# A scan with a mixture of adapters on one core: the store of chunks 68 and 69 from two DMA queues

## The chip, the cores and the metric

The kernel runs on one core of a Trainium2 chip. The metric is the time of one execution on the device in microseconds (us), less being better. SyncE (SP) issues the DMAs; 16 DMA engines move the data between HBM and the on-chip memory SBUF. TensorE (PE) multiplies, VectorE (DVE), ScalarE (ACT) and GpSimd (POOL) do the rest.

## The reference

Two inputs of 8 sequences x 6400 steps x 128 channels go through a linear recurrence along the steps, and each of the 51,200 resulting rows through a mixture of 8 low-rank adapters, of which the two with the largest logits count:

```python
for t in range(S):                      # a, b: (8, 6400, 128)
    h = a[:, t] * h + b[:, t]
    x[:, t] = h
logits = x @ w_gate                     # x as (51200, 128), w_gate (128, 8)
topk = argpartition(-logits, 2)[:, :2]
w = softmax over the two chosen logits
out = x + sum over the chosen e of  w_e * ((x @ A[e]) @ B[e])     # A (8, 128, 16), B (8, 16, 128)
```

Inputs and output are 32-bit floats. `a` and `b` are 26.2 MB each, the output is 26.2 MB.

## The kernel before, in words

The rows are cut into 100 chunks of 512 rows. A chunk is `J` = 4 blocks of 128 rows. The stages of a chunk:

- **Load** (`load`, line 710): SyncE loads `a` and `b` for two chunks at once, 512 KB a DMA, into six pairs of buffers `a_tm` and `b_tm`. A buffer is loaded again when TensorE has read it.
- **Front** (`front`, lines 731, 749, 787): TensorE transposes `a` and `b` so that the channels lie on the partitions, ACT copies the transposed `a` to `a_st`, and DVE runs the recurrence as a scan into `xT`. The scans are one chain from chunk to chunk.
- **Logits** (`zlogits`, lines 807 and 813): TensorE multiplies six blocks (a unit) by the gate and by all the adapters' A side by side; ACT copies the result to `zl`.
- **Gating** (`gating`, lines 844 to 883): for a group of up to four units, GpSimd and DVE find the two largest logits, ACT takes the sigmoid (877) and DVE writes the weights `g` (883).
- **Back** (`back_part`): GpSimd (916) (for chunks 82, 84, 86 and 90 to 99 DVE, 920) multiplies `zl` by `g` into `zw`; TensorE transposes it (929); DVE or ACT copies it (938, 935); TensorE adds x and the adapters' output in PSUM (943, 944); ACT (958), for chunks 95 and 97 DVE (955), copies the sum to `outt`.
- **Store** (`store`, line 989): SyncE stores two chunks at once, 512 KB, from `outt`; the last four chunks go one by one, 256 KB each.

`outt` holds `NO` = 72 blocks, that is 18 chunks; chunk 86 writes where chunk 68 lay, and `olast` tells it which store it has to wait for.

No engine decides its order when it runs. A planner in the program (`Program.schedule`) simulates the five queues with an estimated duration for each operation, due times (`NUDGE`, a table of ranks by the operation's name) and the time of an issue (`ISSUE`), and fixes one order for each engine; where no operation that is due can go on, it takes the earliest that is ready. `Program.waits` then places the semaphore waits, and each engine works through its list in order.

A store is one DMA over 128 partitions, with 4 KB of each partition for two chunks. `SPLIT` makes an exception of the store that begins with chunk 68: `cuts` lists the numbers of partitions of its parts, `lows` where each begins, and `send` issues one DMA for each on SyncE, all with the same semaphore (`parts` counts them). At its end SyncE waits for the semaphores of the stores (`final`).

Of the kernel before, what the change touches and what calls it, by code (L numbers as in the profile page):

```python
# [10 lines left out]
PERIOD = 6  # L11
# [6 lines left out]
LAND_MARGIN = 1.0  # L18
Q_RATE = {3: 4.2e-3, 5: 2.1e-3, 7: 2.1e-3}
SCAN_SELF = 0.13  # L20
ISSUE = {"sp": 0.52, "act": 0.45}
LOAD_RATE = 387e3
STORE_RATE = 413e3
DMA_START = 0.3
# [191 lines left out]
}  # L216
WINDOW = {'pe': 0.0, 'act': 0.0, 'dve': 0.0, 'pool': 0.0, 'sp': 0.0}
START = (-999, "", 0)
# [22 lines left out]
NO = 72  # L241
TAIL = 0
STORE_TAIL = [1, 1, 1, 1]
SPLIT = {68: [124, 4]}
TOP8 = 4
TEMPLATE = {
    "la": [0.0, 0.0, 0.0],
# [50 lines left out]
class Program:  # L298
# [34 lines left out]
    def schedule(self):  # L333
# [17 lines left out]
        while any(queue.values()):  # L351
# [35 lines left out]
            else:  # L387
                free[e] = t + ISSUE[e]
                dma = max(dma, free[e] + DMA_START) + op.dur
# [57 lines left out]
def bass_associative_scan_2x2__then__mixture_of_adapters_kernel(  # L447
# [14 lines left out]
    J = C // 128  # L462
# [50 lines left out]
    for u0, n in groups:  # L513
        nb = sum(m for _, m in units[u0 : u0 + n])
        if pos + nb > NZ:
            pos = 0
        for u in range(u0, u0 + n):
            zpos[u] = pos
            pos += units[u][1]

    with ExitStack() as stack:
# [48 lines left out]
        P = Program()  # L570
        eng = {}

        def sem(name):
            return sb(nc.semaphore(name))
# [4 lines left out]
        def dma_sem(key):  # L579
            if key not in s_dma:  # L580
                s_dma[key] = sem("s_" + key)
            return key
# [11 lines left out]
        for key, dur, dst, src in (  # L594
# [6 lines left out]
                START, sem=dma_sem(key),  # L601
# [19 lines left out]
        def place_pick():  # L621
            with nc.allow_low_precision(reason="sums of a single one"):
# [18 lines left out]
                op=ALU.mult),  # L641
# [15 lines left out]
        o_la, o_lb, o_A, o_B, o_ae, o_sc = {}, {}, {}, {}, {}, {}  # L657
        o_Z, o_ze, o_mu, o_T, o_te, o_D, o_oe, o_st = {}, {}, {}, {}, {}, {}, {}, {}
        o_g = {}
        zlast, xlast, olast = {}, {}, {}  # L660

        def get(d, k):
            return [(d[k], True)] if k in d else []
# [238 lines left out]
        def back_part(gi, ch, c, b0, n):  # L902
# [45 lines left out]
            xlast[ch % NX] = o_D[c]  # L948
            o0 = b0 % NO
            freed = {olast[o0 + k].i: olast[o0 + k] for k in range(n) if o0 + k in olast}  # L950
            deps = [(o_D[c], True)] + [(x, True) for x in freed.values()]
            ov, bv = outt[:, o0 : o0 + n, :].rearrange("p k w -> p (k w)"), bank[:, 0 : n * 128]
            if c in OE_DVE:
# [4 lines left out]
                                lambda: eng["act"].copy(ov, bv), ba(gi, c, "oe"))  # L958
            for k in range(n):
                olast[o0 + k] = o_oe[c]  # L960

        def place(c):
            turn = c - (NCH - TAIL_CHUNKS)
            if turn < 0:
                return pO[:, c % 2, :], get(o_oe, c - 2)
            assert NCH - 1 in o_sc
            t = turn % 6
            if turn < 6:
                if t < 2:
                    free = get(o_oe, c - 2)  # L970
                elif t < 4:
                    free = get(o_ae, NCH - 2 + (NCH + t) % 2)
                else:
                    free = get(o_sc, NCH - 2 + (NCH + t) % 2)
            else:
                free = get(o_oe, c - 6)
            return (pO[:, (c if t < 2 else t) % 2, :] if t < 2 else (pA if t < 4 else pB)[:, t % 2, :]), free

        def store(c, m):
            q = c * J % NO  # L980
            r0 = rows[c]
            src = {olast[q + k].i: olast[q + k] for k in range(m * J)}
            dst = out[r0 : r0 + m * C, :].rearrange("(h p j) d -> p h j d", p=128, j=J)
            view = outt[:, q : q + m * J, :].rearrange("p (h j) d -> p h j d", j=J)
            cuts = SPLIT.get(c, [128])
            lows = [sum(cuts[:i]) for i in range(len(cuts))]

            def send():
                all = [eng["sp"].dma_start(dst[p : p + n], view[p : p + n]) for p, n in zip(lows, cuts)]
                return all if len(all) > 1 else all[0]  # L990

            op = P.add(
                "sp", f"st{c}", m * C * D * 4 / (STORE_RATE if m == 2 else LOAD_RATE), [(x, True) for x in src.values()],
                send, (PERIOD * (c // PERIOD), "st", c % PERIOD // 2),
                sem=dma_sem(f"st{q // (2 * J)}" if m == 2 else f"stx{c % 4}"), parts=len(cuts),
            )
            o_st[c] = op
            for k in range(m * J):
                olast[q + k] = op
# [20 lines left out]
        for gi, (u0, n) in enumerate(groups):  # L1020
            for u in range(u0, u0 + n):
                b0, m = units[u]
# [31 lines left out]
        @block.sync  # L1054
        def _(sp):
            run("sp", sp)
            final = {}
            for op in P.order["sp"]:
                if op.sem.startswith("st"):
                    final.pop(op.sem, None)  # L1060
                    final[op.sem] = op
            for key in final:
                sp.wait_ge(s_dma[key], 16 * sum(o.parts for o in o_st.values() if o.sem == key))

# [43 lines left out]
```

## Time and profile before

| What | Value |
|---|---|
| median of 3 runs | 203.14 us (202.98 to 203.28) |
| the profiled execution's own time | 202.69 us |
| its span, first to last instruction of the program | 200.7 us |
| busy: PE, DVE, ACT, GpSimd | 90%, 88%, 86%, 70% |
| SyncE's DMA queue, share of 16 engines' span | 99.2% |
| moved over the span | 79.26 MB, 395 GB/s |
| DMAs of GpSimd's queue | none |

The profile is of one execution. Its views are: the page (busy shares, 40 slices, DMA queues, the chain that ended last, the costliest groups, the DMA issues), tables of stretches of the span, the order of time of each engine with what ended its idle time, the instructions of one line with the time from a DMA's issue to its landing, and the waits. PEld is TensorE's weight load, L958 means line 958 of the kernel. A DMA issue is time of the issuing queue, not of the transfer.

### The profile page before, as it was taken

What the parts mean: (1) busy time and instruction counts of PE and PEld (TensorE: products, weight loads), DVE (VectorE), ACT (ScalarE), POOL (GpSimd) and SP (SyncE); (2) the same over time, 40 slices, a digit from 0 to 9 for tenths busy, and PEclk for the clock granted to TensorE, in tenths of its full rate; (3) what the DMA queues carried; (4) which work ended last, traced back from release to release, by engine and by line L of the source; (5) the groups of instructions that cost most, each with busy time, mean ns of one, the idle gap of its engine ahead of it and who ended that gap; (6) DMA issues with size and microseconds to landing.
All of it is one profiled execution on the core that took longest, in us unless ns stands there. A gap on an engine that the chain in (4) does not pass through costs nothing.

```text
span 200.7 us, 7490 instructions
## 1 busy us (share of the span) xinstructions
PE 180.8 (90%) x3128; PEld 157.9 (79%) x3128; DVE 176.5 (88%) x287; ACT 172.7 (86%) x317; POOL 140.5 (70%) x182
## 2 busy tenths in 40 slices
PE   6978999999999999899989999988879999998980
PEld 6868877888788888788878888877767887887860
DVE  1579999999999999999999999987888989999980
ACT  2548898999999998999899998986988998998971
POOL 1314559997888899797989798979678677744200
PEclk9999999999999999999999999999999999999997
DMA  5999999999999999999999999999999999999995
GB/s 213 382 391 389 412 406 411 398 416 407 406 410 414 405 411 412 416 411 407 408 414 408 409 418 407 407 411 414 410 413 411 410 414 410 404 384 379 352 371 225
DMA packets 30089, 79.26 MB, mean 395 GB/s; under 512 B 2664, under 2 KB 2920, under 8 KB 30056
## 3 DMA queue, kind: packets, MB, share of 16 engines
q1 hardware_dynamic: 29480, 78.39, 99.2%
q8 instruction: 25, 0.41, 0.8%
q10 hardware_dynamic: 576, 0.40, 0.6%
q14 instruction: 8, 0.07, 0.1%
HBM read 52.56 MB, written 26.21 MB: 393 GB/s over the span
## 4 chain that ended last, share of the span: by engine, by line
PE 21%; DVE 18%; DMA 13%; POOL 7%; ACT 3%; issue 2%; SPq 0%; DVEq 0%
DVE xT L787 9%; DMA b_tm<-in_b_dram 7%; DMA a_tm<-in_a_dram 6%; PE pZ L807 4%; POOL zw L916 4%; PE pA L731 4%; PE pB L731 3%; PE pO L929 3%; DVE zw L920 3%; PE pO L943 3%; PE pO L944 3%; DVE zwT L938 2%; ACT zl L813 1%; POOL L L846 1%; DVE g L883 1%
## 5 line engine op out<-in xcount | busy, mean ns | idle before, releaser
L787 DVE TENSOR_TENSOR_SCAN xT<-a_st,xT,pB 128x512 f16<-128x512 f32 x96 | 120.3, 1253 | 7.8 <-PE pB L731 3.7
L916 POOL TENSOR_TENSOR zw<-zl,g 128x512 f16<-128x512 f32 x87 | 92.0, 1068 | 21.9 <-DVE g L883 18.8
L731 PE MATMUL pB<-ident_f,b_tm 64*128 64x64 f32 (+1 forms) x752 | 68.3, 232 | 2.1 <-DMA a_tm<-in_a_dram 1.0
L731 PE MATMUL pA<-ident_f,a_tm 64*128 64x64 f32 (+1 forms) x752 | 68.2, 232 | 1.7 <-DMA b_tm<-in_b_dram 1.3
L749 ACT COPY a_st<-pA 128x512 f32<-128x512 f32 x100 | 59.9, 608 | 8.3 <-PE pA L731 5.9
L731 PEld LDWEIGHTS pA<-ident_f,a_tm 64*128 64x128 f32 (+1 forms) x752 | 55.7, 140 | 6.8 <-DMA b_tm<-in_b_dram 2.4
L813 ACT COPY zl<-pZ 128x816 f32<-128x816 f32 (+1 forms) x69 | 57.8, 838 | 3.7 <-PE pZ L807 3.5
L731 PEld LDWEIGHTS pB<-ident_f,b_tm 64*128 64x128 f32 (+1 forms) x752 | 55.2, 139 | 7.0 <-DMA a_tm<-in_a_dram 1.7
L958 ACT COPY outt<-pO 128x512 f32<-128x512 f32 x91 | 54.3, 609 | 3.3 <-PE pO L944 2.6
L943 PE MATMUL pO<-ident_h,xT 128*128 128x128 f16 x368 | 51.0, 221 | 0.5 <-ACT zwT L935 0.2
L944 PE MATMUL pO<-cst_h,zwT 128*128 128x128 f16 x368 | 50.3, 219 | 0.0
L943 PEld LDWEIGHTS pO<-ident_h,xT 128*128 128x128 f16 x368 | 40.7, 113 | 2.5 <-ACT zwT L935 0.4
L807 PE MATMUL pZ<-cst_h,xT 128*128 128x136 f16 x400 | 36.0, 225 | 6.4 <-ACT zl L813 2.7
L929 PE MATMUL pO<-ident_h,zw 128*128 128x128 f16 x368 | 35.5, 220 | 2.1 <-ACT outt L958 1.3
L944 PEld LDWEIGHTS pO<-cst_h,zwT 128*128 128x128 f16 x368 | 36.5, 99 | 0.0
L807 PEld LDWEIGHTS pZ<-cst_h,xT 128*128 128x128 f16 x400 | 26.3, 115 | 11.6 <-DVE xT L787 4.3
L938 DVE COPY zwT<-pO 128x512 f16<-128x512 f16 x72 | 29.2, 408 | 2.4 <-PE pO L929 2.0
L929 PEld LDWEIGHTS pO<-ident_h,zw 128*128 128x128 f16 x368 | 22.6, 97 | 6.2 <-issue 1.5
L846 POOL TENSOR_SCALAR L<-k 128x192 f32<-128x192 f32 (+2 forms) x15 | 12.2, 810 | 3.2 <-DVE k L844 2.0
L935 ACT COPY zwT<-pO 128x512 f16<-128x512 f16 x20 | 11.9, 603 | 1.3 <-PE pO L929 1.0
L787 DVE TENSOR_TENSOR_SCAN xT<-a_st,pB 128x512 f16<-128x512 f32 (+1 forms) x8 | 7.5, 937 | 4.9 <-ACT a_st L749 4.7
L853 POOL TENSOR_TENSOR L<-k,m 128x192 f32<-128x192 f32 (+2 forms) x17 | 8.5, 500 | 2.5 <-DVE m L851 2.4
(56 smaller groups left out, 110.8 us busy)
## 6 DMA issues: line engine op xcount, KB each, us to landing
a_tm<-in_a_dram SPq DMA_DIRECT2D x48, 512.0 KB, 13.2
b_tm<-in_b_dram SPq DMA_DIRECT2D x48, 512.0 KB, 13.3
out_dram<-outt SPq DMA_DIRECT2D x47, 512.0 KB, 13.4
a_tm<-in_a_dram SPq DMA_DIRECT2D x4, 256.0 KB, 4.2
out_dram<-outt SPq DMA_DIRECT2D x4, 256.0 KB, 3.6
b_tm<-in_b_dram SPq DMA_DIRECT2D x3, 256.0 KB, 4.8
out_dram<-outt SPq DMA_DIRECT2D x1, 496.0 KB
b_tm<-in_b_dram ACTq DMA_DIRECT2D x1, 256.0 KB, 3.5
```

Of the source, the lines that this page charges most:

```text
L731: last = eng["pe"].transpose(*args)
L749: lambda: eng["act"].copy(a_st[c % NA][:, :], pA[:, c % 2, :]), fr(c, "ae"))
L787: last = eng["dve"].tensor_tensor_scan(out=x[:, s0:s1], data0=a_st[c % NA][:, s0:s1], data1=pB[:, c % 2, s0:s1], initial=init, op0=ALU.mul ...
L807: last = eng["pe"].matmul(pZ[:, k // (n // 2), o : o + W], xblock(b0 + k), Awg_h)
L813: return eng["act"].copy(zl[:, zb : zb + n, :].rearrange("p (h k) w -> p h (k w)", h=2), pZ[:, :, 0 : n // 2 * W])
L846: lambda e: e.tensor_scalar(out=ll, in0=kk, scalar1=0.0, scalar2=-1.0e30, op0=ALU.is_ge, op1=ALU.mult))
L916: lambda: eng["pool"].tensor_tensor(out=wv, in0=zv, in1=gv, op=ALU.mult), ba(gi, c, "mu"))
L929: last = eng["pe"].transpose(ptile[:, k * 128 : k * 128 + 128], zz[:, k, :], ident_h[:, :])
L938: lambda: eng["dve"].tensor_copy(zt, ptile[:, 0 : n * 128]), ba(gi, c, "te"))
L943: eng["pe"].matmul(dst, xblock(b0 + k), ident_h[:, :], start=True, stop=False)
L944: last = eng["pe"].matmul(dst, zt[:, k * 128 : k * 128 + 128], B_h, start=False, stop=True)
L958: lambda: eng["act"].copy(ov, bv), ba(gi, c, "oe"))
```

## The change

The pair of chunks 68 and 69, 512 KB, went out from SyncE as two DMAs over partitions 0 to 123 and 124 to 127. Now SyncE stores partitions 0 to 67 in one DMA, and a new operation `sw68` on GpSimd stores partitions 68 to 81 and 82 to 127 in two DMAs. `sw68` waits for the same copies as the store, has the same rank in the plan (102.531 above the same base) and a semaphore of its own; the planner books 2.6 us for the transfer and 1.3 us of GpSimd's time. A new table `oside` lets the chunk that writes the same blocks of `outt` next wait for this operation too, and SyncE waits for its semaphore at the end. The rest of the diff is the table `NUDGE` with the one new entry, wrapped anew.

```diff
-ISSUE = {"sp": 0.52, "act": 0.45}
+ISSUE = {"sp": 0.52, "act": 0.45, "pool": 1.3}
...
+    ... "sw68": 102.531, ...
...
-SPLIT = {68: [124, 4]}
+SPLIT = {68: [68]}
+ASIDE = {68: [14, 46]}
...
-        zlast, xlast, olast = {}, {}, {}
+        zlast, xlast, olast, oside = {}, {}, {}, {}
...
             freed = {olast[o0 + k].i: olast[o0 + k] for k in range(n) if o0 + k in olast}
+            freed.update({oside[o0 + k].i: oside[o0 + k] for k in range(n) if o0 + k in oside})
...
             for k in range(n):
                 olast[o0 + k] = o_oe[c]
+                oside.pop(o0 + k, None)
...
             cuts = SPLIT.get(c, [128])
             lows = [sum(cuts[:i]) for i in range(len(cuts))]
+            if c in ASIDE:
+                p0 = sum(cuts)
+                views = []
+                for n in ASIDE[c]:
+                    views.append((dst[p0 : p0 + n], view[p0 : p0 + n]))
+                    p0 += n
+                side = P.add(
+                    "pool", f"sw{c}", 2.6, [(x, True) for x in src.values()],
+                    lambda: [eng["pool"].dma_start(d, v) for d, v in views], (PERIOD * (c // PERIOD), "st", c % PERIOD // 2),
+                    sem=dma_sem(f"sw{c}"), parts=len(views))
+                o_st[-c] = side
+                for k in range(m * J):
+                    oside[q + k] = side
...
+            for op in P.order["pool"]:
+                if op.sem is not None:
+                    final[op.sem] = op
```

58 rows, old and new, of the table NUDGE are left out of this document.

## The prediction

> **What bounds the kernel now.** I read the page first: the busy shares and the DMA rows (section 1 to 3), then the DMA issues (6).
>
> ```profile
> span 200.7 us, 7490 instructions
> PE 180.8 (90%) x3128; PEld 157.9 (79%) x3128; DVE 176.5 (88%) x287; ACT 172.7 (86%) x317; POOL 140.5 (70%) x182
> q1 hardware_dynamic: 29480, 78.39, 99.2%
> out_dram<-outt SPq DMA_DIRECT2D x47, 512.0 KB, 13.4
> out_dram<-outt SPq DMA_DIRECT2D x4, 256.0 KB, 3.6
> out_dram<-outt SPq DMA_DIRECT2D x1, 496.0 KB
> out_dram<-outt SPq DMA_DIRECT2D x1, 16.0 KB
> ```
>
> SyncE's queue (q1) fills the 16 DMA engines for 99.2% of the span: the kernel moves data nearly all the time. The last two rows are the store of chunks 68 and 69 in its two parts, 124 and 4 partitions; unlike the other stores they have no landing time behind them. The view gives one only where a semaphore got sixteen updates for each DMA. The updates themselves are in the trace, but no view lists them, so they have no row: this semaphore got 10 from these two DMAs, of which 8 come at 178.6 to 181.2 us, four and four, and two at the issues. I read that as 124 = 4 x 31 and 4 = 4 x 1: each of the two parts ran on four engines, where 128 partitions run on all 16.
>
> Then the end, by stretches of the span (the last two columns are the share of the 16 DMA engines that is busy, and GB/s) and by the issues and landings of the last four stores.
>
> ```profile
> 158.00:166.00 8.00, 7.38 (x144) 6.35 (x141) 6.97 (x11) 7.42 (x14) 6.11 (x8) 1.00 1.03 409
> 182.00:186.00 4.00, 3.26 (x50) 2.70 (x47) 3.77 (x13) 3.73 (x10) 1.13 (x2) 1.00 0.98 376
> 186.00:190.00 4.00, 3.74 (x60) 3.40 (x60) 3.83 (x20) 4.00 (x10) 0.96 (x5) 1.00 0.90 342
> 194.00:197.30 3.30, 1.85 (x24) 1.16 (x20) 1.23 (x3) 2.33 (x4) 0.00 (x0) 1.00 0.85 323
> 197.30:199.00 1.70, 0.00 (x0) 0.00 (x0) 0.00 (x0) 0.00 (x0) 0.00 (x0) 0.63 0.82 313
> 199.00:200.70 1.70, 0.00 (x0) 0.00 (x0) 0.00 (x0) 0.00 (x0) 0.00 (x0) 0.50 0.17 64
> 196.02 0.59 ACT outt L958
> L989 SPq DMA_DIRECT2D out_dram<-outt x1: 351/351/351, 194.6 to 194.6; - x1
> DMA to landing us min/median/max: 3.7/3.7/3.7
> L989 SPq DMA_DIRECT2D out_dram<-outt x1: 854/854/854, 195.3 to 195.3; - x1
> DMA to landing us min/median/max: 3.7/3.7/3.7
> L989 SPq DMA_DIRECT2D out_dram<-outt x1: 1078/1078/1078, 196.2 to 196.2; - x1
> DMA to landing us min/median/max: 3.4/3.4/3.4
> L989 SPq DMA_DIRECT2D out_dram<-outt x1: 564/564/564, 197.3 to 197.3; - x1
> DMA to landing us min/median/max: 2.9/2.9/2.9
> ```
>
> The last copy (ACT L958) ends at 196.02 + 0.59 = 196.61, the last store is issued at 197.3 and lands at 197.3 + 2.9 = 200.2; the span ends 0.5 us later. The four landings are 198.3, 199.0, 199.6 and 200.2: a step of (200.2 - 198.3) / 3 = 0.63 us. One of these stores is 256 KB, 16 KB (16,384 bytes) for each engine, and at 409 / 16 = 25.6 GB/s for one engine that is 0.64 us. So the engine that lands last works without a break to the end: the bytes that it has left set the end, and the 0.7 us by which the last issue trails the last copy is hidden behind them. At the same time the share is 0.90, 0.85 and 0.82, so other engines are idle. The end belongs to a few late engines, which began the tail with more to do than the rest. The question of this change is who they are and what the new split gives them.
>
> **The change part by part.** *Bytes.* The pair is 512 KB, 4 KB a partition. Before, by the reading above, each of four engines gets 31 + 1 = 32 partitions, 128 KB or 131,072 / 25.6e3 = 5.1 us, and twelve get none. After, SyncE sends 68 partitions (68 = 4 x 17: 68 KB, 2.7 us each on four engines, 60 KB or 2.4 us less than before) and GpSimd's queue 14 + 46 = 60 partitions. No row shows a DMA from GpSimd. Its bounds on one engine are nothing and, for 46 partitions carried as 2 x 23, 92 KB or 3.7 us on each of two engines; the 14 would be one partition each, 4 KB or 0.16 us, on fourteen engines. Even spreading of the 60 over 16 is up to 4 partitions, 16 KB, 0.64 us for each. I take the first form, 2 x 23 and 14 x 1, as that is how the 124 behaved in this trace.
>
> The Trainium skill, "DMA: Bandwidth & Descriptors", section "Why a DMA increments its semaphore by 16 and not by 1", says the same for both queues: the largest count up to 16 that divides the slowest dimension, on SyncE's queue the lowest-numbered engines and on GpSimd's consecutive ones from a cursor that goes round. By it the 14 take engines 0 to 13 from a cursor at 0, and the 46 take 14 and 15. It adds an exception, in which GpSimd's DMAs take ceil(partitions / 16) on each engine, and a row on engines 7 and 15 being usually slower; no run here shows either.
>
> *Who was late.* The sixteen updates of the store before this one (issued 166.4; again without a row) come at 173.6 to 179.7: four within 0.3 us, three up to 175.1, two at 176.5 and 177.0, six at 178.2 to 178.4 and the last alone at 179.7. So some engines were 5 to 6 us ahead and one was 1.3 us behind the next, before the four got their 128 KB. Reading the following stores, the four that carried it were among the first seven; they join the late one, and at the end three or four engines land within 0.1 us at 200.2. Taking 2.4 us off the four therefore leaves the one that was late anyhow: it had none of the 512 KB, and it cannot get less. It gets 0 or 4 KB more: **0 to +0.16 us**, of which I take 0.16, since 14 of 16 engines would get such a piece.
>
> *SyncE's queue.* Two issues become one.
>
> ```profile
> 166.91 0.48 SPq L989 DMA_DIRECT2D out_dram<-outt  x1
> 167.43 1.76 SPq L989 DMA_DIRECT2D out_dram<-outt  x1
> 169.24 2.88 SPq L989 DMA_DIRECT2D out_dram<-outt  x1
> L989 SPq DMA_DIRECT2D out_dram<-outt x1: 372/372/372, 186.1 to 186.1; - x1
> 184.54 0.57 ACT L958 COPY outt<-pO 128x512 f32<-128x512 f32 x1
> ```
>
> An issue without congestion takes 0.37 us (the fourth row); these take up to 2.88 because the queue is full, so a dropped issue moves the wait to the next one. What follows in the queue are stores only, all loads went before. The buffer of chunks 68 and 69 is written next by chunk 86 (ACT at 184.54; its store goes at 186.1), 3.3 us after the last of the updates at 181.2, and the later buffers have similar room: **0**, unless the GpSimd part landed over 3 us later than now.
>
> *GpSimd.* The operation sw68 waits for the copies of chunks 68 and 69 and puts two DMAs into an engine that works in order. Behind it are the products zw (L916) and the gating of the next group, which releases ACT's sigmoid and DVE's g (L883), and DVE is the engine of the tail.
>
> ```profile
> 153.51 0.59 ACT L958 COPY outt<-pO 128x512 f32<-128x512 f32 x1 [0.50 <-PE pO L944]
> 156.92 3.09 POOL L916 TENSOR_TENSOR zw<-zl,g 128x512 f16<-128x512 f32 x3 [1.74 <-DVE g L883]
> 161.73 0.52 POOL L844 TENSOR_TENSOR k<-zl,m 128x192 f32<-128x192 f32 x1 [1.72 <-DVE m L862]
> 167.71 0.59 POOL L875 TENSOR_TENSOR k<-k,L 128x192 f32<-128x192 f32 x1
> 169.22 2.09 POOL L916 TENSOR_TENSOR zw<-zl,g 128x512 f16<-128x512 f32 x2 [0.92 <-DVE g L883]
> L916 POOL TENSOR_TENSOR zw<-zl,g x87: 1052/1062/1607, 16.8 to 182.1; 128x512 f16<-128x512 f32 x87
> ```
>
> Counted back from the last copy, chunk 69's is the first row, done at 154.1. GpSimd then sits idle for 1.74 us before 156.92 and 1.72 us before 161.73; from there to 168.3 it is busy nearly without a gap up to k of L875, which g waits for. The price of one issue lies between 0.37 us (SyncE's) and 1.6 us (the longest product of GpSimd), so two cost 0.7 to 3.2 us; the planner in the code books 1.3 for the operation's hold on the engine. I take 2 x 1.3 = 2.6 us, nearer to the engine's own rows. In an idle stretch 1.7 of it is covered and 0.9 is left; inside the busy stretch nothing is. DVE would feel that in full, but the end would not: the last store is issued 0.7 us after its copy because the issue before it takes 1.08 us, and that much delay is free. So 0.9 - 0.7 = 0.2 us at most from an idle stretch, and 2.6 - 0.7 = 1.9 us from the busy one. As the operation is ready by 154, I take the idle stretch, and as the products there have more than 3 us until their copies, **0**.
>
> The Trainium skill, "SBUF — State Buffer", section "Who interferes with whom", warns that GpSimd can be locked out of writing descriptors by certain DVE operations. The 87 products have a median of 1062 ns and a longest of 1607, so what this trace shows of such disturbance is 0.5 us once; by the rule the two issues could take longer than I book.
>
> *Sum.* 0.16 + 0 + 0 = +0.16 us. The profiled execution took 202.69 us, its span of 200.7 and 2.0 around it, 0.45 below the median of 203.14; it would become 202.85. On the median: 203.14 + 0.16 = **203.3 us**. A measurement of this kernel can tell about 0.2%, 0.4 us, from no change, so this counts as the same.
>
> **The rivals.** *A: the two engines of the 46 are not ahead (slower).* The 92 KB need 3.7 us of lead over the late engine. Of the sixteen, seven had over 4 us; nine had not. For an engine of the six, 1.3 us ahead, the end moves by 3.7 - 1.3 = 2.4 us; for the two with 2.7 and 3.2 us by 0.5 to 1.0, for the late one itself by 3.7. It decides as soon as the lead is under 3.7 us. In the middle +1.3: 204.4, at most 206.8. For it: nothing in the views says which engines are ahead, and the 14 partitions ahead of the 46 look neutral to it. Against: four light engines were hit by the 124, so the light ones seem to lie together. By the skill's row on engines 7 and 15 the late engine could be one of the two, the worst end of this rival.
>
> *B: GpSimd's DMAs spread evenly (slower by a little; the change then doesn't do what its numbers suggest).* Up to 4 partitions on the late engine: +0.64 us, 203.8. That is also the skill's exception.
>
> *C: GpSimd's two issues fall into the busy stretch (slower).* +0.2 to +1.9 us, in the middle 204.2. It decides when over 0.7 us reaches DVE. Against: the copies are done by 154 and two idle stretches follow.
>
> *D: the late engine is late because of the four (faster).* Then 2.4 us less on them frees the end until the last copy binds: issue at 196.65 instead of 197.3 saves 0.65 us, and a landing without a step of backlog another 0.64: -0.65 to -1.3 us, in the middle 202.2. For it: the share falls below 1 only after the four got their load, and they are among the last at the end. Against: the spread before the split.
>
> **How the numbers follow.** Forecast 0.35; A 0.24, B 0.09, C 0.10, D 0.22. The range reaches from the middle of D, 202.2, to 205.0, which holds B, C without its far end and A up to an engine with 1.8 us of lead; outside are A's worst and D's best, under 0.2 together. The forecast's own range is 202.9 to 203.5. Faster by over 0.2%: D, 0.22. Within 0.2%: the forecast, 0.35. Slower: A, B and C, 0.43.
>
> **What would show it.** Right: a queue of GpSimd's with 240 KB in section 3, the 272 KB store without a landing time, the last four landings again about 0.63 us apart and ending at 200.2 to 200.5, shares under 1 in the stretches from 182 us. A: landings after 200.7 with the last store issued at its old time, and loads that land later if the operation goes early. B: the late step of 0.6 us, with no two engines standing out. C: GpSimd's L875 of the group later than 167.71 and DVE's scans behind it. D: the last issue 0.04 us after its copy and a landing under 2.9 us. I am wrong on the main point if the last landing moves earlier by over 0.4 us, since by my reading no byte leaves the late engine.

## The result: 7.6 us slower, and the profile after

| | before | after |
|---|---|---|
| median (runs) | 203.09 us (202.98 to 203.28, 4) | 210.67 us (210.46 to 210.74, 4) |
| ratio, 95% interval | | 1.037 (1.035 to 1.039) |
| the profiled execution: own time, span | 202.69, 200.7 us | 210.74, 208.5 us |
| mean granted clock of TensorE | 0.993 | 0.982 |

The forecast was 203.3 us, the range up to 205.0: wrong, and by far. The kernel before ran again on the same chip beside each group of experiments; its medians were 203.2 to 203.5, and each difference below is against the one beside it. Ratios leave out runs that look disturbed by their clock; as in this kernel the clock falls because of its own gaps, all runs are listed where a group of them splits.

The page of after, and its table of DMAs:

```profile
span 208.5 us, 7488 instructions
PE 183.2 (88%) x3128; PEld 158.9 (76%) x3128; DVE 178.5 (86%) x287; ACT 173.2 (83%) x317; POOL 143.0 (69%) x184
q1 hardware_dynamic: 29356, 78.15, 95.5%
q0 software_dynamic: 416, 0.25, 0.4%
out_dram<-outt SPq DMA_DIRECT2D x4, 256.0 KB, 2.4
out_dram<-outt SPq DMA_DIRECT2D x1, 272.0 KB
out_dram<-outt POOLq DMA_DIRECT2D x1, 184.0 KB, 10.9
out_dram<-outt POOLq DMA_DIRECT2D x1, 56.0 KB, 5.7
```

q0 is GpSimd's queue. Its packets (in the trace, in no view) are 60 of 4 KB, 32 of 4 bytes and 324 of 8 bytes. The 56 KB DMA lands on all its engines within 0.9 us; in the other, two engines land at 167.6 and 167.8, 2 us behind the rest. So the split was as forecast: 14 single partitions, and 46 as 2 x 23, 92 KB on each of two engines. The small packets fit: 2 engines without any of the 14, one packet each, and 14 without any of the 46, 23 each, are 2 + 322 = 324. SyncE's queue (q1) no longer fills the span: 95.5% after 99.2%. Where it runs empty, by stretches (columns: PE, PEld, DVE, ACT, GpSimd busy with their instructions, clock, DMA share, GB/s):

```profile
158.00:166.00 8.00, 7.53 (x148) 6.71 (x147) 7.43 (x10) 7.20 (x13) 6.26 (x8) 1.00 1.04 406
182.00:186.00 4.00, 3.91 (x70) 3.31 (x71) 3.97 (x9) 4.00 (x10) 1.96 (x2) 1.00 0.92 347
186.00:190.00 4.00, 3.18 (x43) 2.44 (x43) 3.99 (x13) 3.53 (x8) 2.78 (x5) 1.00 0.48 187
190.00:194.00 4.00, 3.76 (x63) 3.39 (x62) 4.00 (x13) 3.78 (x9) 0.00 (x0) 1.00 0.61 230
194.00:198.00 4.00, 3.81 (x61) 3.24 (x58) 3.96 (x14) 3.33 (x9) 1.75 (x5) 1.00 0.47 179
202.00:205.22 3.22, 1.10 (x16) 0.76 (x14) 0.37 (x1) 1.59 (x3) 0.00 (x0) 0.85 0.41 151
```

From 186 to 198 us the share is 0.47 to 0.61, with DVE busy nearly all of that time. The end is no longer that of a late DMA engine: the last four stores, issued from 203.9 to 205.2, land at 205.9, 206.6, 207.3 and 208.0, each on all its engines within 0.2 us. Something in the last 50 us makes the engines late.

**Two places.** First the loads. SyncE's issues in before, then in after, and the load of `b` for chunk 92 (the second of each "x2") with the time to its landing:

```profile
151.42 1.80 SPq L710 DMA_DIRECT2D b_tm<-in_b_dram  x2
158.61 1.47 SPq L710 DMA_DIRECT2D a_tm<-in_a_dram  x1
160.12 0.67 SPq L710 DMA_DIRECT2D b_tm<-in_b_dram  x1
```

```profile
L710 SPq DMA_DIRECT2D b_tm<-in_b_dram x1: 596/596/596, 152.6 to 152.6; - x1
DMA to landing us min/median/max: 13.7/13.7/13.7
```

```profile
152.39 1.76 SPq L711 DMA_DIRECT2D b_tm<-in_b_dram  x2
159.43 3.03 SPq L711 DMA_DIRECT2D a_tm<-in_a_dram  x1
162.51 1.92 SPq L711 DMA_DIRECT2D b_tm<-in_b_dram  x1
```

```profile
L711 SPq DMA_DIRECT2D b_tm<-in_b_dram x1: 581/581/581, 153.6 to 153.6; - x1
DMA to landing us min/median/max: 16.1/16.1/16.1
```

The load takes 16.1 us instead of 13.7. Of its sixteen updates fifteen are there by 167.0 in after and the last at 169.7; in before 165.8 and 166.4. One engine is late. As I read it, it is one of the two that work on GpSimd's 4 KB packets until 167 us, in turn with the loads that were queued there before. The next issue hangs too, 3.03 us instead of 1.47. Who feels it in after, from the order of time of ACT, TensorE and DVE:

```profile
166.78 1.07 ACT L960 COPY outt<-pO 128x512 f32<-128x512 f32 x2 [1.13 <-DMA out_dram<-outt]
169.70 0.27 PE L732 MATMUL pA<-ident_f,a_tm 64*128 64x64 f32 x1 [1.32 <-DMA b_tm<-in_b_dram]
166.34 1.28 DVE L788 TENSOR_TENSOR_SCAN xT<-a_st,xT,pB 128x512 f16<-128x512 f32 x1 [0.47 <-PE pA L732]
170.59 1.28 DVE L788 TENSOR_TENSOR_SCAN xT<-a_st,xT,pB 128x512 f16<-128x512 f32 x1 [1.75 <-PE pB L732]
```

ACT waits 1.13 us for an earlier store that sits on the same engine (chunks 56 and 57, whose blocks it writes next), TensorE 1.32 us for the load, and between two scans of DVE's chain lie 4.25 us (before: 2.1). And TensorE's clock, before and after:

```profile
166.00:170.00 4.00, 3.84 (x68) 3.19 (x68) 4.00 (x7) 3.13 (x7) 2.88 (x4) 1.00 1.04 412
170.00:174.00 4.00, 3.81 (x79) 3.31 (x78) 4.00 (x8) 3.98 (x8) 3.04 (x5) 1.00 1.03 402
```

```profile
166.00:170.00 4.00, 1.36 (x27) 0.94 (x24) 2.37 (x4) 1.56 (x3) 2.82 (x5) 1.00 1.03 408
170.00:174.00 4.00, 4.00 (x56) 3.56 (x53) 2.75 (x3) 2.32 (x5) 1.21 (x2) 0.57 1.04 406
```

TensorE is busy in 1.36 of 4 us, and then runs at a mean clock of 0.57 for four. The trace's clock records, which no view lists, have it at 0.50 for one stretch of 3.41 us, from 170.1 to 173.5.

Second, the order. From chunk 77 on, the lists of all five engines differ from before: 30 places on TensorE, 25 on ACT, 41 on DVE, 8 on GpSimd, 2 on SyncE. The new operation's 2.6 us of transfer, booked on the planner's one DMA timeline, move every later landing that it plans with. Planned with 0 us of transfer and 1.3 us of GpSimd's time the order is that of before, and with 2.6 and 0 it is that of after: the transfer alone does it. The 2.6 is also far above what the planner books elsewhere: at its rate for stores (`STORE_RATE`, 413,000 bytes a us) the 240 KB would be 0.6 us, and planned with 0.6 the order is that of before too.

### The profile page after: what moved, and what is told of

Its sections match the earlier page's. It is cut to its first block, busy times and chain, and to the rows that moved or that the text cites. A ratio compares the mean times of both kernels' runs of the same rounds, so it can differ in the third digit from the quotient of the medians.

```text
span 208.5 us, 7488 instructions
## 1 busy us (share of the span) xinstructions
PE 183.2 (88%) x3128; PEld 158.9 (76%) x3128; DVE 178.5 (86%) x287; ACT 173.2 (83%) x317; POOL 143.0 (69%) x184
## 3 DMA queue, kind: packets, MB, share of 16 engines
q1 hardware_dynamic: 29356, 78.15, 95.5%
## 4 chain that ended last, share of the span: by engine, by line
DMA 21%; PE 17%; DVE 10%; ACT 7%; POOL 7%; issue 2%; SPq 1%; ACTq 0%; DVEq 0%
DMA b_tm<-in_b_dram 14%; DMA a_tm<-in_a_dram 7%; DVE xT L788 5%; POOL zw L917 4%; PE pZ L808 3%; PE pA L732 3%; PE pB L732 3%; PE pO L944 3%; PE pO L945 2%; PE pO L930 2%; ACT outt L960 2%; DVE zw L921 2%; ACT a_st L750 2%; ACT zl L814 1%; DVE zwT L939 1%
## 5 line engine op out<-in xcount | busy, mean ns | idle before, releaser
L944 PE MATMUL pO<-ident_h,xT 128*128 128x128 f16 x368 | 51.8, 222 | 1.1 <-ACT zwT L936 0.5
L945 PE MATMUL pO<-cst_h,zwT 128*128 128x128 f16 x368 | 51.0, 220 | 0.0
L808 PE MATMUL pZ<-cst_h,xT 128*128 128x136 f16 x400 | 36.5, 227 | 5.4 <-ACT zl L814 2.7
L808 PEld LDWEIGHTS pZ<-cst_h,xT 128*128 128x128 f16 x400 | 26.8, 115 | 10.6 <-DVE xT L788 4.6
```

Of the source, the lines that this page charges most:

```text
L808: last = eng["pe"].matmul(pZ[:, k // (n // 2), o : o + W], xblock(b0 + k), Awg_h)
L944: eng["pe"].matmul(dst, xblock(b0 + k), ident_h[:, :], start=True, stop=False)
L945: last = eng["pe"].matmul(dst, zt[:, k * 128 : k * 128 + 128], B_h, start=False, stop=True)
```

## The experiments

Three theories: ORDER (the new lists are slower), LOADS or ENGINES (the lump of 92 KB on two engines makes loads land late), START (a DMA of GpSimd's costs time at the start). In names such as T79 the letter is the operation (T the transposes of `zw`, P those of a chunk's `a` and `b`, `oe` the copy to `outt`, `te` the copy to `zwT`), the number the chunk.

**One cause at a time.** The order of before with the stores of after:

```diff
-        P.schedule()
+        P.schedule(); at = [o.name for o in P.order["pool"]].index("mu75"); P.order["pool"][at:at] = [o for o in P.ops if o.name.startswith("sw")]
...
```

(`mu75` is GpSimd's product of chunk 75. Two more lines, left out here, keep `sw68` out of the planning.)

> The planner's order of before on every engine, with the three stores of after (68 from SyncE, 14 and 46 from GpSimd, put ahead of the product of chunk 75 as in after). Theory ORDER (the new operation made the planner write another order for all engines from chunk 77 on, and that order is what is slow): most of the 7.6 us is gone; what is left is the 1.0 us offset of the start and about 2 us by which the last loads land late: 204.5 to 206. Theory ENGINES (23 partitions on each of two DMA engines make the last loads land 2.8 us late, and the tail magnifies that whatever its order): 209 to 211. Theory START (a queue of GpSimd's costs 1.0 us at the start): the first scans and stores are 1.0 us later than in before, here too.

Measured: 207.22, 207.29, 206.87 and 204.08 us, two levels, to which I come back. And the reverse, the order of after with the stores of before (sw68 is planned and then left out; `SPLIT = {68: [124, 4]}`):

> The planner's order of after on every engine, but GpSimd's operation is left out when the order stands, and SyncE issues 124 and 4 partitions as in before: no DMA from GpSimd. ORDER: about 5 us of the 7.6 stay, 207 to 209. ENGINES: 202.8 to 203.6, as before. START: the start is as in before, no 1.0 us offset.

Measured: 206.13 us (206.07 to 206.27), ratio 1.0142 (1.0118 to 1.0167): the new order alone costs 2.65 us, with no DMA from GpSimd and the loads landing as before (last 177.0, before 176.9). Neither theory alone holds the 7.6. How the order loses it, before and this kernel (ACT, then DVE):

```profile
169.12 0.59 ACT L958 COPY outt<-pO 128x512 f32<-128x512 f32 x1
169.61 0.84 ACT L813 COPY zl<-pZ 128x816 f32<-128x816 f32 x1
170.34 0.60 ACT L958 COPY outt<-pO 128x512 f32<-128x512 f32 x1
172.80 1.27 DVE L787 TENSOR_TENSOR_SCAN xT<-a_st,xT,pB 128x512 f16<-128x512 f32 x1
174.56 1.27 DVE L787 TENSOR_TENSOR_SCAN xT<-a_st,xT,pB 128x512 f16<-128x512 f32 x1
```

```profile
169.72 0.84 ACT L813 COPY zl<-pZ 128x816 f32<-128x816 f32 x1 [0.30 <-PE pZ L807]
171.29 1.08 ACT L958 COPY outt<-pO 128x512 f32<-128x512 f32 x2
172.42 1.06 POOL L916 TENSOR_TENSOR zw<-zl,g 128x512 f16<-128x512 f32 x1 [0.88 <-PE pO L929]
174.51 0.35 DVE L851 TENSOR_REDUCE m<-L 128x24 f32<-128x192 f32 x1 [0.49 <-POOL L L849]
174.78 1.27 DVE L787 TENSOR_TENSOR_SCAN xT<-a_st,xT,pB 128x512 f16<-128x512 f32 x1
176.29 1.27 DVE L787 TENSOR_TENSOR_SCAN xT<-a_st,xT,pB 128x512 f16<-128x512 f32 x1
```

The copies 77 and 76 stand behind other copies now and come one after the other from 171.29, instead of at 169.12 and 170.34; T79 needs the space in pO that they free, GpSimd waits for T79 0.88 us, DVE for GpSimd, and the same two scans come 2.0 and 1.7 us later. Is that first step a loss of its own? A plan with 1.3 us of transfer changes 17 places around it, and nothing later:

> No DMA of GpSimd, stores of before (124 and 4). The order is that which the planner writes when it books 1.3 us of transfer for the new operation instead of 2.6: 17 places differ from before, all around chunks 77 to 85 (TensorE: T79 behind the transposes of chunk 94; ACT: each of the copies 77 and 76 one place later; DVE: te79 two scans later), and the order after them is that of before. Theory FIRST STEP (the copies 77 and 76 that come 2.2 and 1.4 us late take pO from T79 and so the DVE chain; this loss is carried to the end): +1.5 to +2.0 over before, 204.6 to 205.5. Theory ALL OF IT (the 3 us of the new order come from the many changes in the last 20 us): under +0.5, 203.0 to 204.0.

Measured: 205.01 us (204.31 to 206.29), +1.8, ratio 1.0077 (1.0050 to 1.0103). FIRST STEP: by the medians two thirds of the order's 2.65 us. But the two slowest of the nine runs, 205.92 and 206.29, have the lowest clock (0.986 and 0.984). In the profiled one of them, 205.92, TensorE's clock falls behind the sparse stretch that the order makes, with no DMA from GpSimd:

```profile
170.00:174.00 4.00, 2.42 (x43) 1.73 (x41) 3.93 (x7) 2.79 (x6) 2.68 (x4) 1.00 1.03 405
174.00:178.00 4.00, 4.00 (x57) 3.60 (x54) 2.32 (x5) 2.80 (x5) 1.58 (x2) 0.57 1.03 394
```

Without these two the median is 204.68 us: the first step itself is nearer to 1.5 us, a little over half of the order's loss.

**The lump.** GpSimd's two DMAs in the other order, `ASIDE = {68: [46, 14]}`:

> As the first kernel of this call (order of before), but GpSimd stores 46 partitions first and then 14. If the DMA engines are dealt from a cursor, the 2 x 23 partitions now fall on other engines than in after. ENGINES: if the two are among those that run ahead, the loads land as in before, and the time is 203 to 204.5, clearly under the first kernel's; if they are late ones too, 209 to 211. ORDER: 203 to 206, within 2 us of the first kernel.

204.34 us (203.80 to 205.32), ratio 1.0051 (1.0028 to 1.0074): no lone late engine, the last load at 177.0. The same 60 partitions as one DMA, `ASIDE = {68: [60]}`:

> As the first kernel of this call (order of before), but GpSimd stores the 60 partitions in one DMA; 60 = 15 x 4, so 15 engines would carry 16 KB each instead of two 92 KB. ENGINES: the last load is at most 0.64 us late, 203 to 204.5. ORDER: the same, since only the 92 KB lump is gone and the order is that of before: 203 to 204.5. The difference to the first kernel is the price of the lump with the order unchanged: 0 to 2 us by ORDER, 5 to 7 us by ENGINES.

203.58 us, ratio 1.0009 (0.9985 to 1.0033): in this order no price can be measured, with GpSimd's DMA still there. It is the lump on two engines and, as I read the kernel before this one, which two; the trace does not number the engines.

Later in GpSimd's list, the lump meets few loads:

> Order of before, the three stores of after (68; 14 and 46), but GpSimd issues its two behind the product of chunk 83 instead of ahead of that of chunk 75, some 15 us later. Theory LOADS (the two 92 KB lumps cost time because their packets take half of an engine that still has loads queued): the last load lands as in before, within 0.5 us, and what is left is GpSimd's 1.9 us in a stretch with little idle time and the late engines' last stores: 203.8 to 205.5. Theory END (the lump costs its 3.7 us wherever it falls, at the end through the late engine's stores): 206.5 to 207.5, as with the early issue in the order of before.

204.79 us (204.57 to 205.43), ratio 1.0074 (1.0052 to 1.0095). The load of chunk 92 takes its 13.7 us again and the last one lands at 177.2: LOADS. The +1.6 left are GpSimd's issues in its busy stretch and late last stores; they were not taken apart. All parts from SyncE, `SPLIT = {68: [68, 14, 46]}`:

> Order of before; all three parts, 68, 14 and 46 partitions, from SyncE, which issues them behind the last load. LOADS: the loads land as in before whatever engines the lumps fall on; if they fall on the engines that carry the 68 anyhow (17 + 23 + 1 partitions, 164 KB on two of them against 128 KB before), these are ahead and 203.0 to 204.0 comes out. END: as the lump is there in full, 205 or more.

205.28 us, ratio 1.0098 (1.0063 to 1.0133), outside my 203 to 204: the loads are as in before (177.1), but one engine is 1.7 us behind the rest to the end and lands the last store at 202.7. So END has its share here, as I read it because the lump falls on SyncE's own four engines.

**The sum.** The kernel of after with 0 instead of 2.6 us booked, the same program as the first experiment:

> The kernel of after with one number changed: the planner books 0 instead of 2.6 us of transfer for the new operation. That alone gives back the order of before on every engine (GpSimd's 1.3 us stay booked). The program is that of the order of before with the new stores, whose four runs lay apart (204.08, and 206.87 to 207.29); this settles which is its time. ORDER and LOADS together (3.6 us each): 206.5 to 207.5, with now and then a run near 204 if the lump sometimes meets engines that are ahead. ORDER alone: 203.5 to 204.5 in nearly all runs.

205.04, 208.03, 204.39, 207.20, 206.99 and 208.46 us; ratio without the two of lowest clock 1.0128 (1.0079 to 1.0178). And the new order with GpSimd's 60 partitions in one DMA:

> The order of after (2.6 us booked), but GpSimd stores its 60 partitions in one DMA, so that no engine gets 92 KB. If the two causes add, what is left is the new order alone: 206.0 to 206.8, as with the stores of before in this order (206.13). If the new order is only slow because of a DMA from GpSimd at that place, 208 or more; if the lump was the whole cause, 203.3 to 204.

207.22 us (206.68 to 207.85), ratio 1.0183 (1.0159 to 1.0207), 0.4 above what was expected and +3.8 on before. So in this order even the one DMA is not free: the time is 1.1 us above that of the order alone, chunk 92's load takes 14.4 us instead of 13.7 there, and the last load lands at 178.5 instead of 177.0. By itself the order costs 2.65 us, and the lump, by the medians of two scattered sets of runs, 3.6 to 3.7. Together that is 6.2 to 6.4 of the 7.6 us; the other 1.2 to 1.4 come only with both, and no run takes them apart.

But why are there two groups of runs of one program? With the first experiment: 204.08 to 205.04 at clocks of 0.997 to 1.000, and 206.87 to 208.46 at 0.975 to 0.991. In the profiled run of 207.22 the load of chunk 92 lands after 16.7 us, and the clock falls; in that of 205.04 it lands after 14.6 us, and there is no drop of the clock:

```profile
166.00:170.00 4.00, 1.28 (x20) 0.85 (x18) 2.37 (x4) 1.56 (x3) 1.73 (x3) 0.94 1.05 410
170.00:174.00 4.00, 4.00 (x60) 3.56 (x58) 2.46 (x3) 2.80 (x6) 1.48 (x3) 0.63 1.02 401
```

```profile
166.00:170.00 4.00, 2.66 (x50) 2.22 (x51) 3.21 (x6) 2.15 (x5) 2.33 (x4) 1.00 1.03 408
170.00:174.00 4.00, 3.81 (x74) 3.33 (x72) 4.00 (x8) 3.98 (x8) 3.08 (x4) 1.00 1.04 412
```

TensorE is busy in 2.66 of 4 us, not in 1.28. What makes the lump hold up chunk 92's load less in one run than in another stays open: in both, GpSimd's DMA lands late (167.3 and 167.8 us), and so does the last load (179.8 and 179.3).

**The clock.** Transposes that nobody uses, to keep TensorE busy where it waits:

```diff
+        at = [o.name for o in self.order["pe"]].index("P94"); self.order["pe"][at:at] = [o for o in self.ops if o.name.startswith("fx")]
...
+        for k in range(12):
+            P.add("pe", f"fx{k}", 0.109, [(o_id, True), (o_sc[92], True)],
+                  lambda: eng["pe"].transpose(pB[:, 0, 0:128], ident_f[:, :], ident_f[:, :]), START)
```

> The kernel of after, unchanged but for 12 transposes of the identity into a free half of pB that TensorE runs ahead of the transposes of chunk 94, where it waits 1.3 us for the late load and where its clock then falls to 0.53 and 0.62 for four us. They keep TensorE busy and compute nothing that is used. Theory CLOCK (a good part of what the late loads cost is the clock that falls behind TensorE's idle time): the clock stays at 1.00 from 170 to 174 us and the time falls by 1.0 to 1.8 us, to 208.9 to 209.7. Theory WAIT (the late landing alone sets it): 210.4 to 211.5.

> As the one before this, with 24 instead of 12 of these transposes. CLOCK: the clock stays up and the time is that of 12 plus what the longer row of transposes delays TensorE beyond the landing, 0 to 1.3 us: 208.9 to 211.0. If 12 are too few to hold the clock, 24 do: under the time of 12. WAIT: 211 to 212.

> The order of before with the new stores, and 12 such transposes ahead of those of chunk 94. Without them, in two calls, two groups of runs: 204.08, 204.39 and 205.04 at a granted clock of 0.997 to 1.000, and 206.87 to 208.46 at 0.975 to 0.991. CLOCK: the upper group comes down by 1.0 to 1.8 us, so most runs lie from 204.5 to 206.0 and the clock of all is over 0.993. WAIT: the groups stay, with 207 the most frequent.

209.66 (208.82 to 210.72), 212.93 (210.37 to 214.16) and 208.00 us (207.28 to 208.22). These don't test the theory: I had put the transposes ahead of chunk 94, but the wait is that of chunk 92, so they ran behind the gap, and in the profiled runs the clock fell to 0.50 to 0.59 over two us, as in after. That the first median lies in the range that CLOCK had is an accident of two levels: 208.82 and 209.03 us at clocks of 0.992 and 0.996, 210.29 and 210.72 at 0.986. At the gap:

```diff
-            P.add(..., [(o_id, True), (o_sc[92], True)], ...
+            P.add(..., [(o_id, True), (o_sc[90], True)], ...   # 11 ahead of T76, 11 ahead of chunk 92
```

> The kernel of after with 22 transposes of the identity that nobody uses, this time at the gap itself: 11 ahead of the transposes of zw of chunk 76, where TensorE waits 1.2 us for ACT, and 11 ahead of chunk 92's, where it waits 1.3 us for the late load (the three kernels before had them ahead of chunk 94's, behind the gap). CLOCK: the clock stays at 1.00 from 170 to 174 us and the time falls by 0.8 to 1.8 us, to 208.9 to 209.9. WAIT: 210.4 to 212.0.

> The order of before, the new stores, and the same 22 transposes at the same two places. Without them 204.08 to 205.04 at a clock over 0.995 and 206.87 to 208.46 under 0.992. CLOCK: the clock stays up in all runs, which lie from 204.3 to 206.3. WAIT: most runs stay at 207 to 208.5.

209.25 us (208.51 to 209.43), ratio 1.0273 (1.0255 to 1.0291), and 205.45 us (204.81 to 205.85), ratio 1.0095 (1.0079 to 1.0112). The first of them:

```profile
166.00:170.00 4.00, 3.56 (x40) 3.01 (x38) 2.37 (x4) 1.56 (x3) 1.67 (x3) 1.00 1.04 410
170.00:174.00 4.00, 3.64 (x76) 3.16 (x72) 3.11 (x5) 3.20 (x6) 1.52 (x2) 1.00 1.03 408
```

The clock stays at 1.00 though the load lands as late as in after (169.4), and with added work the kernel is 1.4 us faster than after, by the ratios (1.0370 and 1.0273) nearer to 2. CLOCK. In the order of before the upper group of runs is gone too, but there the profiled run has the load after 15.3 us instead of 16.7, so it does not show which of the two, the transposes or a less late load, did it. The less late load need not be enough: in the first kernel with transposes it took 15.1 us, and the clock fell. A path from before to after is then: 203.48 (before, beside these runs), 205.45 with the lump, 209.25 with the new order too, 210.67 with the clock free to fall: +2.0, +3.8 and +1.4. Its steps are not clean. A part of the +3.8 can be the later load (16.7 us in the profiled run of 209.43), as the order by itself costs 2.65. The 210.67 is from the first runs, beside which before had 203.09, and what the transposes themselves cost is within the +2.0.

**Another split?** Was the 124 and 4 of before worth something, and does one like it help the loads?

> Order of before, no split: the store of chunks 68 and 69 is one DMA over 128 partitions. What is the split of before worth? If the four engines that carried its 124 partitions are ahead and the others late, the others now get 32 KB = 1.28 us more behind the last load: the last landing 1.3 us later, up to 204.5. If the end is bound by the copies, 203.0 to 203.5. The loads land as in before in both cases.

> Order of before, no DMA of GpSimd. The store of chunks 60 and 61, which is queued ahead of the last loads, goes out as 124 and 4 partitions too. If the engines that carry the 124 are ahead there as they are with chunk 68, the late engines get 32 KB less ahead of the last five loads, which land up to 1.3 us earlier: 201.8 to 203.0. If they are not ahead, or the tail's order can't use earlier loads: 203.5 to 206.

> Order of before, its 124 and 4 for chunk 68, and the store of chunks 60 and 61, which is queued ahead of the last five loads, as 120 and 8 partitions: 120 = 15 x 8, so by the rule of the divisor one engine carries nothing of it and the others 32 or 36 KB. In before the sixteenth update of each of the last loads comes 0.8 to 1.0 us behind the fifteenth. If that late engine is the one that is left out, the last loads land up to 1.0 us earlier, and 202.2 to 203.0 comes out. If it is another, it gets 4 KB more or nothing: 203.0 to 203.8.

> As the kernel before this in the call, with the store of chunks 56 and 57 as 120 and 8 too. If the late engine is the one left out: it is 2.6 us lighter, the other late ones set the loads, and the gain is at most that of one split, 202.0 to 203.0. If it is another: 203.0 to 204.0.

One DMA: 203.76 us, ratio 1.0010 (0.9990 to 1.0031), so the split of before has no worth that can be measured. 124 and 4 also for chunk 60: 207.86 us, ratio 1.0212 (1.0174 to 1.0251): the lump on SyncE's four engines makes the load's issue at 158.73 take 3.83 us, the last load lands at 178.1 us, and the last store's landings lie 4 us apart; so those four were not ahead by what they were given. With 120 and 8: 203.59 and 203.62 us, ratios 1.0002 (0.9983 to 1.0021) and 1.0007 (0.9987 to 1.0026). There the first landing of the late loads comes 0.9 and 1.9 us earlier and the last as before (177.0 and 177.3), so the engine left out is an early one. Nothing here beats the kernel before.

**START** fell: SyncE's fourteenth load of `a` is issued at 22.44 us in before and at 23.59 in after, but kernels without a DMA of GpSimd's have 22.45 to 22.96 and those with it 22.50 to 23.38. What makes the start vary stays open; of the 7.8 us between the two profiled spans it may be up to 1.2.

## Why the prediction was wrong, point by point

**The sum had no term for the order** (2.65 us by itself). "The change part by part" prices bytes, SyncE's queue and GpSimd's time against the lists of before. That the planner writes the lists from the durations it books was known from the code, and the diff adds two of them. I weighed the 1.3 as a price of the chip and took the 2.6 us of booked transfer for nothing, where it rewrote the tail. No rival held it either.

**"Who was late" looked at the end only.** The bytes were right, 92 KB on two engines and 4 KB on fourteen. But "the late engine keeps its load" asks what each engine has left at 200 us, from landings of 173 to 180 us, and GpSimd's packets ran from 160 to 167, while the last six loads were on the same engines. There a load is complete when its last engine is, and the copy, the transposes and the scan wait for it. Rival A had the fact, engines that are not ahead, and the wrong place: it priced them by the last store, +0.5 to +3.7. What the runs showed is a load 2.4 to 3.0 us late, TensorE without work, and its clock falling behind that: 3.6 to 3.7 us for the lump by itself. That this is near A's worst, 3.7, is chance, as the loads played no part in it.

**SyncE's queue at 0**: its step "all loads went before" is true of SyncE's part (272 KB, issued at 169.6), and was never asked of GpSimd's, issued at 156.1 and 156.9, ahead of the last four loads. The room in the buffer was looked up for chunk 86 and held; what failed was chunk 74's copy, which waits for an earlier store on the late engine.

**GpSimd at 0** held:

```profile
155.58 0.59 POOL L876 TENSOR_TENSOR k<-k,L 128x192 f32<-128x192 f32 x1
156.12 1.90 POOL L998 DMA_DIRECT2D out_dram<-outt  x2
158.05 3.10 POOL L917 TENSOR_TENSOR zw<-zl,g 128x512 f16<-128x512 f32 x3
```

Two issues took 1.90 us, 0.95 each within my 0.37 to 1.6, and fell into the idle stretch; the products begin 0.27 us behind the g that they wait for, instead of 0.08. Rival C did not happen, nor was the lock-out by DVE seen: the second issue took 1.13 us, about as long as one of GpSimd's products (1.06).

**The end** did not stay with the late DMA engine: the last landing moved by 7.8 us because the engines were late, and the queue ran dry in front of it. Rivals B and D did not happen; the even spread of B, brought about by one DMA of 60 partitions, costs 0.1 us in the order of before, within the noise.

## What to carry to other kernels

Where a planner writes the order, an added operation can change all that stands behind it: compare the two lists of each engine before pricing anything, look at what the new durations are booked on, and whether they are at the rates of the rest. A DMA from another queue does not stand behind the loads of the first; what it puts on one engine delays what is already queued there, and a load is as late as its last engine. And in a stretch where TensorE is barely kept busy (here 1.36 of 4 us), waits of 1.2 to 1.3 us can cost its clock besides.

## What was not expected of the hardware

- A queue does not shield its DMAs: loads issued at 152.4 to 154.2 us were held up by a DMA issued at 156.9 from GpSimd, whose packets on the two engines ran from about 162 to 167 us. The Trainium skill, "DMA: Bandwidth & Descriptors", section "Queues, rings and completion order", says that an engine goes round between the queues that it has work for; the trace agrees, 16.1 us for the load instead of 13.7.
- TensorE's clock halved (0.50 for 3.41 us, from 170.1) with no wait of its matmuls above 1.32 us, after a stretch with 1.36 us of work in 4. The Trainium skill, "TensorE: Matmul & The Clock Gate", section "HAM oscillation — how this bites in real kernels", gives the rule as no idle gap over some 3.4 us; here it was a sparse stretch, not one gap, and 22 transposes in it that nobody uses kept the clock at 1.00. From 40 to 196 us the clock records of the profiled runs have one such stretch, of 3.41 us at 0.50, in six kernels and none in the others, and one of the six has only the first step of the new order and no DMA from GpSimd.
- GpSimd's DMA is slow to begin: its first packet moves 4.0 us after the issue (160.1 for 156.1), and 3.9 to 4.6 us in all twelve profiled runs that have one. It sends packets of 8 bytes too, 324 of them beside the 60 of data, and 4 beside 60 where the 60 partitions go in one DMA. Both counts fit one packet of 8 bytes, on each engine without data, for every partition that an engine with data carries: 2 x 1 + 14 x 23, and 1 x 4.
